# Four heads of num in the 64x64 quadrants of TensorE: a linear-attention and MLP kernel on one core

## The chip, the cores and the metric

The kernel runs on one core of a Trainium2 chip. The metric is the device time of a run in microseconds; lower is better. Times are medians over several runs, and a kernel is always timed in turns with the kernel before on the same chip.

Engine names in the profile: PE is TensorE (matmul), PEld its weight loads, DVE is VectorE, ACT is ScalarE, POOL is GpSimd, SP the engine that issues the output and spread DMAs. TensorE writes its results to `ps_all`, which the kernel divides into eight banks of 512 columns that are used in turn.

## The reference

In short form:

```python
batch, n_heads, seq, head_dim = 8, 8, 576, 64          # n_tokens 4608, d_model 512, d_ff 2048

def phi(x):
    return np.where(x > 0, x, np.exp(x) - 1.0) + 1.0
q_p, k_p = phi(q), phi(k)
kv  = einsum('bhsd,bhse->bhde', k_p, v)
z   = sum(k_p, axis=2)
num = einsum('bhsd,bhde->bhse', q_p, kv)
den = einsum('bhsd,bhd->bhs', q_p, z)[..., None] + 1e-06
x   = (num / den) -> [4608, 512]

h = x @ w_in
g = h - tanh(h)
out = g @ w_out                                        # float32, [4608, 512]
```

## The kernel before

The tokens are worked in nine chunks of 512. A chunk has a first dense layer (sixteen steps `s1` of four 128x128x512 matmuls) and a second (sixteen steps `s2` of four). The attention of a later batch is threaded between these steps. Batch 0 comes before chunk 0 in a prologue; batch 1 runs inside chunk 0, batch 2 inside chunk 1, and so on to batch 7 in chunk 6.

num of a pair of heads is one full 128x128 matmul: the two heads' kv stand as diagonal blocks of a 128x128 stationary operand, so half of the array multiplies zeros. Four matmuls of 512 columns and four of 64 (the last 64 of 576 tokens) make up a batch.

```python
    def load_wi(g):
        f0 = g * (DF // 4)
        nc.gpsimd.dma_start(out=w_in_sb[:, :, f0:f0 + DF // 4],
                            in_=moe_w_in[:, f0:f0 + DF // 4].rearrange("(ko ki) f -> ki ko f", ki=128))
    # ... (cut)
    def num_mm(b, p, banks):
        kz, qT = kz_t[b], qT_t[b]
        ps = banks().rearrange("p (j t) -> p j t", j=8)
        if p < NP:
            nc.tensor.matmul(ps, kz[:, p // 2, p % 2, 0:128], qT[:, p % 2, 0:8, p // 2, :], start=True, stop=True)
        else:
            for a in range(NP):
                nc.tensor.matmul(ps[:, a, :], kz[:, a // 2, a % 2, 0:128], qT[:, a % 2, 8, a // 2, :],
                                 start=True, stop=True)
        return ps
    # ... (cut: a_num multiplies a bank by the spread reciprocal rdb on VectorE; banks 6 and 7 in turn)
    def a_spread_pe(b, bank0, pairs):      # the spread of batches 0 and 1: selector times reciprocal, in fp32
        bp = ps_all[:, bank0:bank0 + 4, :]
        for n, p in enumerate(pairs):
            for t in range(4):
                r = slice(32 * t, 32 * t + 32)
                nc.tensor.matmul(bp[:, t, 144 * n:144 * n + 144], sel[r, p].rearrange("p h e -> p (h e)"),
                                 rden_t[b][r], start=True, stop=True)
        return bp
    # ... (cut)
    load_k(0); load_q(0); load_v(0)        # GpSimd's stream, in order
    make_identity(nc, ident)
    for g in range(4):
        load_wi(g)
    nc.gpsimd.memset(sel, 0.0)             # the selector of the spread
    for t in range(4):
        nc.gpsimd.affine_select(out=sel[32 * t:32 * t + 32], ...)
    load_k(1); load_wo(0); load_q(1); load_wo(1); load_v(1); load_wo(2); load_wo(3)
    # ... (cut: 36 matmuls of zeros, 0.43 us apart before the first clock record
    # at 6.09 us, 0.22 after it; phi of batch 0)
    a_qT_pe(0, 0, side)                    # transposes of q
    a_kv_half(0, 0, kvb)
    a_qT_pe(0, 1, side)
    a_kv_half(0, 1, kvb)
    a_den(0, Banks([0]))                   # ends in the reciprocal on VectorE
    ns0 = a_num_copy(0, Banks([1, 4, 5, 6, 7]))
    bp_a = a_spread_pe(0, 0, (0, 1))
    bp_b = a_spread_pe(0, 4, (2, 3))
    for p in range(NP):
        a_scale(0, p, ns0, (bp_a, bp_b)[p // 2], 144 * (p % 2))     # x = num * spread reciprocal
    # ... (cut) for batches 2 to 7, in the second layer of a chunk:
            for p in range(NP + 1):
                s2[9 + p].append(lambda p=p: a_num(n1, p))
```

kv runs in 64x128 tiles, den in 128x32 tiles and the spread in 32x128 tiles, so the array is already cut up there. The spread copies each token's reciprocal of den to the 64 rows of its head: for batches 0 and 1 by these matmuls, for later batches by DMA through DRAM.

Of the kernel before, what the change touches and what calls it, by code (L numbers as in the profile page):

```python
# [11 lines left out]
F32 = mybir.dt.float32  # L12
# [6 lines left out]
def kernel(  # L19
# [9 lines left out]
    nc = tc.nc  # L29
    B, H, S, D = q.shape  # L30
    N = B * S
    DM = H * D
    DF = moe_w_in.shape[1]
    NP = H // 2
    NF = DF // 128
    NC = N // 512
    J = S // 64
# [8 lines left out]
    rpool = ctx.enter_context(tc.tile_pool(name="rpool", bufs=2))  # L46
# [16 lines left out]
    attn = Banks([6, 7])  # L63
# [43 lines left out]

    def load_wi(g):
        f0 = g * (DF // 4)
        nc.gpsimd.dma_start(out=w_in_sb[:, :, f0:f0 + DF // 4],  # L110
                            in_=moe_w_in[:, f0:f0 + DF // 4].rearrange("(ko ki) f -> ki ko f", ki=128))

    def load_wo(g):
        nc.gpsimd.dma_start(out=w_out_sb[:, 4 * g:4 * g + 4, :],
# [28 lines left out]
            out=qT_t[b].rearrange("p i j g t -> p (i j) (g t)"),  # L143
            in_=qp_t[b].rearrange("p i j h d -> p (i j h d)"))

    def a_qT_pe(b, i, banks):
        if i == 0:
            new_qT(b)
        for n, (j0, j1) in enumerate(((0, 5), (5, 9))):
            ps = banks().bitcast(BF16).rearrange("p (j t) -> p j t", t=128)  # L150
            for j in range(j0, j1):
                nc.tensor.transpose(ps[:, j - j0, :], qp_t[b][:, i, j].rearrange("p h d -> p (h d)"), ident)  # L152
            src = ps[:, 0:j1 - j0, :]
            dst = qT_t[b][:, i, j0:j1].rearrange("p j g t -> p j (g t)")
            if n == 0:
                nc.scalar.copy(dst, src)
            else:
                nc.vector.tensor_copy(dst, src)
# [17 lines left out]
    def a_kv_half(b, i, banks):  # L176
        if i == 0:
            kz_t[b] = work.tile([128, 2, 2, 160], BF16, name="kz")
        ps = [banks()[:, 0:192] for hg in range(2)]
        kv_mm(b, i, ps)  # L180
        for hg in range(2):
            nc.vector.tensor_mul(kz_t[b][:, hg, i, :], ps[hg][:, 0:160], mask[:, hg, i, :])
# [30 lines left out]
                in_=ds[4 * hh:4 * hh + 4].rearrange("h t c -> (h t c)").partition_broadcast(64))  # L213
        rdb_t[b] = rdb

    def num_mm(b, p, banks):
        kz, qT = kz_t[b], qT_t[b]
        ps = banks().rearrange("p (j t) -> p j t", j=8)
        if p < NP:
            nc.tensor.matmul(ps, kz[:, p // 2, p % 2, 0:128], qT[:, p % 2, 0:8, p // 2, :], start=True, stop=True)  # L220
        else:
            for a in range(NP):
                nc.tensor.matmul(ps[:, a, :], kz[:, a // 2, a % 2, 0:128], qT[:, a % 2, 8, a // 2, :],
                                 start=True, stop=True)
        return ps

    def a_num(b, p):
        rdb = rdb_t[b]
        ps = num_mm(b, p, attn)
        if p < NP:  # L230
            nc.vector.tensor_mul(  # L231
                xT[:, p, S * b:S * b + 512].rearrange("p (j t c) -> p j t c", j=8, t=4),
                ps.rearrange("p j (t c) -> p j t c", t=4),
                rdb[:, p, :, 0:8, :].rearrange("p t j c -> p j t c"))
        else:
            nc.vector.tensor_mul(
                xT[:, :, S * b + 512:S * b + 576].rearrange("p a (t c) -> p a t c", t=4),
                ps[:, 0:NP, :].rearrange("p a (t c) -> p a t c", t=4), rdb[:, :, :, 8, :])

    def a_num_copy(b, banks):  # L240

        ns = rpool.tile([128, NP, J, 64], F32, name="ns", tag="rdb")
        ps = num_mm(b, NP, banks)
        nc.scalar.copy(ns[:, :, 8, :], ps[:, 0:NP, :])
        if b == 0:
            for p in range(NP):
                num_mm(b, p, banks)
            for p in (0, 2):
                nc.scalar.copy(ns[:, p:p + 2, 0:8, :].rearrange("p a j t -> p a (j t)"),
                               ps_all[:, 4 + p:6 + p, :])  # L250
        else:
            for p in range(NP):
                ps = num_mm(b, p, banks)
                nc.scalar.copy(ns[:, p, 0:8, :], ps)
        return ns

    def a_spread_pe(b, bank0, pairs):

# [7 lines that stand above are left out]
# [60 lines left out]
    for hh in range(2):  # L326
        nc.vector.memset(mask[64 * hh:64 * hh + 64, :, :, 64 * hh:64 * hh + 64], 1.0)
        for p in range(NP):
            m = 128 + 4 * hh + p
            nc.vector.memset(mask[64 * hh:64 * hh + 64, p // 2, p % 2, m:m + 1], 1.0)  # L330
    for i in range(2):
        nc.vector.memset(v_b[i][:, :, 2], 1.0)
# [16 lines left out]
    a_qT_pe(0, 0, side)  # L349
    a_kv_half(0, 0, kvb)  # L350
    a_qT_pe(0, 1, side)
    a_kv_half(0, 1, kvb)
    a_den(0, Banks([0]))
    ns0 = a_num_copy(0, Banks([1, 4, 5, 6, 7]))
    bp_a = a_spread_pe(0, 0, (0, 1))
    bp_b = a_spread_pe(0, 4, (2, 3))
    for p in range(NP):
        a_scale(0, p, ns0, (bp_a, bp_b)[p // 2], 144 * (p % 2))
    load_q(2)
    load_k(2)  # L360
    load_v(2)
# [1 line left out]
    for c in range(NC):  # L363
        gT = gpool.tile([128, NF, 512], BF16, name="gT")
        n1, n2 = c + 1, c + 2
        s1 = {i: [] for i in range(16)}
        s2 = {i: [] for i in range(16)}
        if c == 0:
            side = Banks([4, 5, 6, 7])
            sub = {}  # L370

            def spread1(h):
                sub["bp"] = a_spread_pe(1, 4, (2 * h, 2 * h + 1))
                for p in (2 * h, 2 * h + 1):
                    a_scale(1, p, sub["ns"], sub["bp"], 144 * (p % 2))

            s1[11].append(lambda: a_kphi(1, 0))
            s1[13].append(lambda: a_kphi(1, 1))
            s1[15].append(lambda: a_qphi(1, 0))
            s2[1].append(lambda: a_qphi(1, 1))  # L380
            s2[4].append(lambda: a_qT_pe(1, 0, side))
            s2[5].append(lambda: a_qT_pe(1, 1, side))
            s2[6].append(lambda: a_kv(1, side))
            s2[8].append(lambda: a_den(1, side))
            s2[9].append(lambda: (sub.update(ns=a_num_copy(1, side)), load_v(3)))
            s2[11].append(lambda: spread1(0))
            s2[13].append(lambda: spread1(1))
            s2[14].append(lambda: a_qphi(2, 0))
            s2[15].append(lambda: a_qphi(2, 1))
        elif n1 < B:  # L390
            s1[9 if c == 1 else 5].append(lambda: a_kv(n1, attn))
            s1[11 if c == 1 else 8].append(lambda: (a_den(n1, attn), a_spread(n1)))
            for p in range(NP + 1):
                s2[9 + p].append(lambda p=p: a_num(n1, p))
            if c + 3 < B:
                s1[10].append(lambda: load_v(c + 3))
        if c == 1:
            s1[1].append(lambda: a_kphi(2, 0))
            s1[3].append(lambda: (a_kphi(2, 1), load_k(3), load_q(3)))
            s1[5].append(lambda: a_qT_pe(2, 0, attn))  # L400
            s1[7].append(lambda: a_qT_pe(2, 1, attn))
        if c >= 1 and n2 < B:
            if c > 1:

                s1[0].append(lambda: (gate(gT, 0), load_k(n2), load_q(n2)))
            d = 4 if c == 1 else 2
            s2[d].append(lambda: a_kphi(n2, 0))
            s2[d + 2].append(lambda: a_kphi(n2, 1))
            s2[d + 4].append(lambda: a_qphi(n2, 0))
            s2[d + 6].append(lambda: (a_qphi(n2, 1), a_qT_dma(n2)))  # L410
        if c == 0:

            hs = [ps_all[:, fi, :] for fi in range(4)]
            first = Banks([4, 5, 6, 7, 0, 1, 2, 3])
            for p in range(NP):
                for fi in range(4):
                    l1mm(c, fi, hs[fi], p)
            for fi in range(4):
                l1act(fi, hs[fi], gT)
        for fi in range(4 if c == 0 else 0, NF):  # L420
            h = first() if c == 0 else dense()
            for p in range(NP):
                l1mm(c, fi, h, p)
            l1act(fi, h, gT)
            for f in s1[fi]:
                f()
        os_ = {}
        for s in range(16):

            (g, i) = divmod(s, 4) if c == 0 else (s % 4, s // 4)  # L430
            if g == 0:
                os_[i] = ps_all[:, i, :] if c == 0 else dense()
            l2mm(gT, os_[i], i, 4 * g, 4 * g + 4)
            if g == 3:
                evac(c, i, os_[i])
            for f in s2[s]:
                f()
# [30 lines left out]
```

## Time and profile before

| | |
|---|---|
| median time | 303.05 us (302.71 to 303.22, 3 runs) |
| span of the profiled run, granted clock | 301.5 us, 0.997 |
| TensorE busy | 292.2 us, 97% |
| first dense matmul | 20.06 us |
| num of one batch in the chain | 0.98 us |

The prediction shows the lines that carry the reading. One row of the page that it didn't show matters later: the granted clock in 40 equal slices, in tenths. The first is the row of the profiled kernel before. The second line below is from the view of busy time by stretch: the stretch in us, its length, then busy time and count of PE, PEld, DVE, ACT and POOL, the granted clock, the DMA share and GB/s.

```profile
PEclk9999999999999999999999999999999999999998
```

```profile
16.33:19.74 3.41, 2.93 (x40) 1.89 (x39) 2.21 (x3) 2.30 (x3) 3.33 (x6) 1.00 1.24 207
```

The reader should see that TensorE was busy for 2.93 of the 3.41 us ahead of the first dense matmul, and that the clock stayed full. The last digit of the row is 8 because the clock is recorded at half again from 299.64 us, after the last matmul; a run's mean clock of 0.997 therefore need not mean that any matmul ran slower.

### The profile page before, as it was taken

What the parts mean: (1) busy time and instruction counts of PE and PEld (TensorE: products, weight loads), DVE (VectorE), ACT (ScalarE), POOL (GpSimd) and SP (SyncE); (2) the same over time, 40 slices, a digit from 0 to 9 for tenths busy, and PEclk for the clock granted to TensorE, in tenths of its full rate; (3) what the DMA queues carried; (4) which work ended last, traced back from release to release, by engine and by line L of the source; (5) the groups of instructions that cost most, each with busy time, mean ns of one, the idle gap of its engine ahead of it and who ended that gap; (6) DMA issues with size and microseconds to landing.
All of it is one profiled execution on the core that took longest, in us unless ns stands there. A gap on an engine that the chain in (4) does not pass through costs nothing.

```text
span 301.5 us, 4703 instructions
## 1 busy us (share of the span) xinstructions
PE 292.2 (97%) x1790; PEld 138.7 (46%) x1790; DVE 180.0 (60%) x304; ACT 149.6 (50%) x228; POOL 51.7 (17%) x91
## 2 busy tenths in 40 slices
PE   8989999979999999999999999999999999999993
PEld 3544454444445444544454445444544444444441
DVE  7658944887557854785478556865681467008500
ACT  3637914954735653566256625662562166136420
POOL 8863253051006000600050003000000000000000
PEclk9999999999999999999999999999999999999998
DMA  6999999677879776967787777477108310130033
GB/s 95 193 206 206 205 207 206 171 113 139 214 101 188 147 170 139 152 109 200 142 145 128 192 149 125 85 177 148 38 2 193 71 35 0 37 86 18 2 70 70
DMA packets 36406, 38.23 MB, mean 127 GB/s; under 512 B 14432, under 2 KB 31008, under 8 KB 35616
## 3 DMA queue, kind: packets, MB, share of 16 engines
q0 software_dynamic: 17600, 18.35, 37.7%
q1 hardware_dynamic: 18784, 19.58, 28.9%
q8 instruction: 14, 0.23, 0.3%
q14 instruction: 8, 0.07, 0.1%
HBM read 43.78 MB, written 9.55 MB: 177 GB/s over the span
## 4 chain that ended last, share of the span: by engine, by line
PE 86%; DMA 4%; DVE 3%; ACT 2%; POOL 1%; issue 1%; SPq 0%; DVEq 0%; ACTq 0%; POOLq 0%
PE ps_all L275 39%; PE ps_all L290 38%; PE ps_all L165 4%; DMA out_dram<-osb 2%; PE ps_all L220 2%; DMA qraw<-in_q_dram 2%; ACT e L127 1%; DVE gT L281 1%; PE ps_all L190 1%; ACT osb L295 1%; PE ps_all L152 1%; POOL kraw L85 1%; PE ps_all L263 1%; DVE qp L129 1%; DVE kp L129 1%
## 5 line engine op out<-in xcount | busy, mean ns | idle before, releaser
L290 PE MATMUL ps_all<-w_out_sb,gT 128*128 128x512 bf16 x576 | 131.6, 379 | 0.0
L281 DVE TENSOR_TENSOR gT<-ps_all,th 128x512 bf16<-128x512 f32 x144 | 96.9, 687 | 53.6 <-ACT th L280 53.2
L275 PE MATMUL ps_all<-xT,w_in_sb 128*128 128x512 bf16 x576 | 128.2, 379 | 0.3 <-DVE xT L268 0.3
L280 ACT ACTIVATE th<-ps_all 128x512 f32<-128x512 f32 x144 | 85.2, 599 | 51.5 <-PE ps_all L275 46.8
L275 PEld LDWEIGHTS <-w_in_sb 128*128 128x128 bf16 x576 | 55.3, 98 | 66.6 <-issue 1.3
L290 PEld LDWEIGHTS <-gT 128*128 128x128 bf16 x576 | 55.6, 98 | 65.7 <-issue 0.3
L295 ACT COPY osb<-ps_all 128x512 f32<-128x512 f32 x36 | 21.1, 587 | 79.7 <-PE ps_all L290 59.6
L231 DVE TENSOR_TENSOR xT<-ps_all,rdb 128x512 bf16<-128x512 f32 x24 | 16.4, 689 | 11.8 <-PE ps_all L220 11.8
L104 POOL DMA_DIRECT2D v<-in_v_dram x32 | 19.2, 616 | 19.0 <-PE ps_all L165 6.0
L127 ACT ACTIVATE e<-kraw 128x1152 bf16<-128x1152 bf16 x16 | 18.5, 1165 | 5.3 <-DMA kraw<-in_k_dram 5.3
L129 DVE TENSOR_TENSOR kp<-e,r 128x1152 bf16<-128x1152 bf16 x16 | 12.2, 760 | 14.1 <-ACT e L127 13.0
L127 ACT ACTIVATE e<-qraw 128x1152 bf16<-128x1152 bf16 x16 | 18.4, 1166 | 0.6 <-DMA qraw<-in_q_dram 0.6
L129 DVE TENSOR_TENSOR qp<-e,r 128x1152 bf16<-128x1152 bf16 x16 | 12.1, 758 | 7.8 <-ACT e L127 7.0
L286 POOL COPY g<-gT 1x1 bf16<-1x1 bf16 x4 | 0.7, 176 | 92.9 <-DVE gT L281 92.9
L165 PE MATMUL ps_all<-v,kp 64*128 64x192 bf16 x288 | 13.7, 243 | 0.0
L165 PEld LDWEIGHTS <-kp 64*128 64x128 bf16 x288 | 11.5, 94 | 3.3 <-issue 2.5
L343 PE MATMUL ps_all<-zero 128*128 128x512 bf16 x36 | 10.3, 460 | 1.2 <-DVE zero L302 1.2
L220 PE MATMUL ps_all<-qT,kz 128*128 128x512 bf16 x32 | 11.2, 379 | 0.0
L89 POOL DMA_DIRECT2D kraw<-in_k_dram x14 | 8.7, 628 | 11.0 <-ACT th L280 9.6
L89 POOL DMA_DIRECT2D qraw<-in_q_dram x14 | 8.8, 642 | 6.1 <-DVE r L128 6.1
L268 DVE TENSOR_TENSOR xT<-ns,ps_all 128x576 bf16<-128x576 f32 x8 | 5.6, 749 | 5.2 <-PE ps_all L263 5.2
L174 DVE TENSOR_TENSOR kz<-ps_all,mask 128x320 bf16<-128x320 f32 x14 | 6.2, 486 | 3.7 <-PE ps_all L165 3.7
(46 smaller groups left out, 92.3 us busy)
## 6 DMA issues: line engine op xcount, KB each, us to landing
out_dram<-osb SPq DMA_DIRECT2D x72, 128.0 KB
rdb<-ds SPq DMA_DIRECT2D x12, 576.0 KB
v<-in_v_dram POOLq DMA_DIRECT2D x32, 144.0 KB, 6.4
kraw<-in_k_dram POOLq DMA_DIRECT2D x14, 288.0 KB, 5.1
qraw<-in_q_dram POOLq DMA_DIRECT2D x14, 288.0 KB, 7.0
w_in_sb<-in_moe_w_in_dram POOLq DMA_DIRECT2D x4, 512.0 KB, 10.1
w_out_sb<-in_moe_w_out_dram POOLq DMA_DIRECT2D x4, 512.0 KB, 13.2
kraw<-in_k_dram POOLq DMA_DIRECT2D x4, 144.0 KB, 3.7
```

What stands on the lines that cost most here:

```text
L89: nc.gpsimd.dma_start(out=t[64 * hg:64 * hg + 64].rearrange("p i h j d -> p (i h) (j d)"), in_=src[b, 4 * hg:4 * hg + 4].rearrange("h (p j ...
L104: nc.gpsimd.dma_start(out=v_b[b % 2][64 * hg:64 * hg + 64, i, 0:2].rearrange("p h j d -> p h (j d)"), in_=v[b, h0:h0 + 2].rearrange("h (p ...
L127: nc.scalar.activation(e, x, AF.Exp)
L129: nc.vector.tensor_tensor(store[b][:, i].rearrange("p j h d -> p h j d"), e, r, ALU.min)
L165: nc.tensor.matmul(ps[hg], kp[r, i, j].rearrange("p h d -> p (h d)"), vt[r, i, :, j, :], start=(j == 0), stop=(j == J - 1))
L220: nc.tensor.matmul(ps, kz[:, p // 2, p % 2, 0:128], qT[:, p % 2, 0:8, p // 2, :], start=True, stop=True)
L231: nc.vector.tensor_mul(xT[:, p, S * b:S * b + 512].rearrange("p (j t c) -> p j t c", j=8, t=4), ps.rearrange("p j (t c) -> p j t c", t=4), ...
L275: nc.tensor.matmul(h, w_in_sb[:, p, fi * 128:(fi + 1) * 128], xT[:, p, c * 512:(c + 1) * 512], start=(p == 0), stop=(p == NP - 1))
L280: nc.scalar.activation(th, h, AF.Tanh)
L281: nc.vector.tensor_sub(gT[:, fi, :], h, th)
L290: nc.tensor.matmul(o, gT[:, fi, i * 128:(i + 1) * 128], w_out_sb[:, fi, :], start=(fi == 0), stop=(fi == NF - 1))
L295: nc.scalar.copy(osb, o)
```

## The change

The intent is to use the whole array: kv's two 64x64 blocks of a pair go one above the other in one column half of the array, and those of another pair in the other half, so that four heads run side by side in one pass and num takes two passes of 512 columns where it took four. The outputs then come in another order of heads, so the rows of w_in are regrouped to match, which cuts each of its four loads in two. In the prologue the first half of num goes ahead of the second half of kv. The transposes of batch 2's q in chunk 1 are spread over four steps instead of two. The core of the diff (the mask's index, the splitting of the transposes' helper, `a_num_copy` and the lines that the new ones replace in num are cut):

```diff
     def load_wi(g):
         f0 = g * (DF // 4)
-        nc.gpsimd.dma_start(out=w_in_sb[:, :, f0:f0 + DF // 4],
-                            in_=moe_w_in[:, f0:f0 + DF // 4].rearrange("(ko ki) f -> ki ko f", ki=128))
+        for hg in range(2):
+            nc.gpsimd.dma_start(
+                out=w_in_sb[64 * hg:64 * hg + 64, :, f0:f0 + DF // 4],
+                in_=moe_w_in[256 * hg:256 * hg + 256, f0:f0 + DF // 4].rearrange("(c e) f -> e c f", e=64))
 ...
+    def num_mm(b, i, ps):
+        kz, qT = kz_t[b], qT_t[b]
+        for ii, j0, j1, o in ((i, 0, 8, 0),) if i < 2 else ((0, 8, 9, 0), (1, 8, 9, 64)):
+            for hg in range(2):
+                for hh in range(2):
+                    r, c = slice(64 * hh, 64 * hh + 64), slice(64 * hg, 64 * hg + 64)
+                    nc.tensor.matmul(ps[hh][c, o:o + 64 * (j1 - j0)], kz[r, hg, ii, r],
+                                     qT[r, ii, j0:j1, hg, :], start=True, stop=True)
+    def a_num(b, i):
+        rdb = rdb_t[b]
+        ps = [attn(), attn()]            # both banks 6 and 7
+        num_mm(b, i, ps)
+        # ... one multiplication on VectorE for each bank
 ...
     a_qT_pe(0, 1, side)
+    ns0 = new_ns(0)
+    a_num_copy(0, ns0, 0, side)
     a_kv_half(0, 1, kvb)
     a_den(0, Banks([0]))
-    ns0 = a_num_copy(0, Banks([1, 4, 5, 6, 7]))
-    bp_a = a_spread_pe(0, 0, (0, 1))
-    bp_b = a_spread_pe(0, 4, (2, 3))
+    a_num_copy(0, ns0, 2, Banks([1, 2]))
+    a_num_copy(0, ns0, 1, side)
+    bp_a = a_spread_pe(0, 0, (0,))
+    bp_b = a_spread_pe(0, 4, (1, 2, 3))
 ...
+            def num1():                  # batch 1, in chunk 0
+                sub["ns"] = new_ns(1)
+                for i in (2, 0, 1):
+                    a_num_copy(1, sub["ns"], i, side)
+                load_v(3)
 ...
-            for p in range(NP + 1):
-                s2[9 + p].append(lambda p=p: a_num(n1, p))
+            for i in range(3):
+                s2[9 + 2 * i].append(lambda i=i: a_num(n1, i))
 ...
-            s1[5].append(lambda: a_qT_pe(2, 0, attn))
-            s1[7].append(lambda: a_qT_pe(2, 1, attn))
+            for n in range(4):
+                s1[4 + n].append(lambda n=n: a_qT_pe(2, n // 2, attn, (n % 2,)))
```

## The prediction

> **What bounds the kernel now.** I read the page first (engine shares, chain), then the chain in order of time, then the timelines of TensorE, VectorE and GpSimd over the first 50 us, and last the waits. The page and the waits:

> ```profile
> PE 292.2 (97%) x1790; PEld 138.7 (46%) x1790; DVE 180.0 (60%) x304; ACT 149.6 (50%) x228; POOL 51.7 (17%) x91
> ...
> L220 PE MATMUL ps_all<-qT,kz 128*128 128x512 bf16 x32 | 11.2, 379 | 0.0
> ...
> PE ps_all L152 <- DVE qT L158: 1.1, 1, 1.1
> ```

> TensorE is busy 97% of a 301.5 us span at a granted clock of 0.997, and num (line 220) never waits. The reader should see that VectorE and ScalarE have slack on average, so a microsecond of TensorE time is a microsecond of the kernel, unless it lies where TensorE waits anyway. The chain in order of time says where that is:

> ```profile
> 17.54 0.95 PE ps_all L263 x14
> ...
> 18.59 1.43 DVE xT L268 x2
> ...
> 20.06 13.97 PE ps_all L275 x64
> ...
> 81.35 0.21 PE ps_all L220
> 81.56 0.86 PE ps_all L290 x4
> 82.42 0.22 PE ps_all L220
> ...
> 84.58 0.22 PE ps_all L220
> 84.80 0.86 PE ps_all L290 x4
> 85.66 0.12 PE ps_all L223 x4
> ```

> From 20.06 us to the last dense matmul the chain is TensorE nearly without a break (the exception is around 53 to 63 us in chunk 1, where the page's waits show TensorE waiting for the transposed q of batch 2). A dense 128x512 matmul costs 13.97/64 = 0.218 us of the chain (0.86/4 = 0.215 later). num of one batch costs four times 0.215 plus 0.12 for the four 64-column matmuls: 0.98 us. For the six batches 2 to 7 that is 5.9 us, for batch 1 another 0.98, and batch 0 lies in the prologue. That is everything that the quadrants can halve: about 3.5 us, or 1.1%.

> What the quadrants cost is in the timeline, at the places where the kernel already leaves the full array:

> ```profile
> 42.65 1.90 PE L290 MATMUL ps_all<-w_out_sb,gT 128*128 128x512 bf16 x8
> ...
> 44.48 0.43 PE L190 MATMUL ps_all<-qT,kz 128*32 128x144 bf16 x16
> ...
> 44.85 1.04 PE L290 MATMUL ps_all<-w_out_sb,gT 128*128 128x512 bf16 x4
> ```

> Eight dense matmuls from 42.65 at 0.216 would end their issue at 44.38; the 128x32 matmuls start at 44.48, so 0.09 us goes on entering. Sixteen matmuls of 144 columns in four column tiles are four rounds; at the 2.37 columns a nanosecond of a dense matmul (512 in 0.216 us) a round is 0.061 us, together 0.24. They hold TensorE 44.48 to 44.85 = 0.37. So leaving costs 0.12 to 0.13, and a visit to another tiling about 0.21 us besides its rounds. kv (64x128) gives the same: 1.59 us in the chain for 18 rounds of 0.081 = 1.46 leaves 0.13, with another 0.09 on entry. The four tiles of a round are truly concurrent, with four different moving operands, so I expect the four quadrants to be as well.

> [...]

> **The change part by part.**

> Steady batches 2 to 7. Two full matmuls (0.43 us) become one visit of four concurrent 64x64 matmuls: 0.22 for the round, 0.21 for entering and leaving, minus nothing: 0.42 to 0.43. This is no gain, twice per batch, because the visits stand alone between groups of four dense matmuls. The tail columns now need a third visit: two rounds of 64 columns, 0.03 plus about 0.05[...], plus 0.21: 0.29 us where four full matmuls took 0.12. Per batch 0.43 + 0.43 + 0.29 = 1.15 against 0.98: +0.15 to +0.17; six batches about +0.9 us.

> Chunk 1 (num of batch 2). Each visit now fills both banks 6 and 7 and needs both evicted (2 x 0.67 us on VectorE) before the next, two steps later (8 x 0.216 + 0.43 = 2.16 us). Before, VectorE took its first num of batch 2 at 82.01, 0.8 us after TensorE had begun it, and between the second and third it did 1.2 us of q's phi. With pairs, visit 2's evictions fall at about 84.5 to 85.9 and visit 3 wants bank 7 at 85.6: a stall of about +0.3 us. In chunks 2 to 5 the phi work is two steps earlier and the same reckoning leaves about 0.2 us to spare: 0. The later chunk has no phi: 0.

> Batch 1 (chunk 0). The three parts share one visit: 0.21 + 0.08 + 2 x 0.22 = 0.73 against 0.98, a gain of 0.25. But they go through a ring of four banks, two at a time, in the order 2, 0, 1: part 1 takes the banks of part 2 and must wait for ScalarE's two small copies. These start some 0.24 us after the matmul (now 45.81 to 46.04) and take about 0.2 us each, so part 1 can go some 0.45 us later than it could. Net +0.2 us.

> Prologue. num of batch 0's first half goes in front of kv's second half: its eviction (two copies of 0.6 us) leaves the critical stretch, but kv, den and the reciprocal come some 0.37 us later (one round of 0.22, one more switch). The spread is now split so that only its first quarter stands before the first scale, and the first dense matmul needs banks 0 to 3 free of one scale (0.75 us) instead of two (1.43 us). By TensorE, VectorE and ScalarE alone I get the first dense matmul at about 19.5 instead of 20.06: -0.55 us.

> But w_in's four DMAs become eight of 64 partitions, in GpSimd's stream ahead of the selector of the spread:

> ```profile
> 9.99 3.00 POOL L110 DMA_DIRECT2D w_in_sb<-in_moe_w_in_dram  x4
> ...
> 12.97 0.56 POOL L311 MEMSET sel<- 128x512 f32 x1
> ...
> 13.61 2.84 POOL L314 TENSOR_SCALAR_AFFINE_SELECT sel<-sel 32x512 f32<-32x512 f32 x4
> ...
> 17.51 0.95 PEld L263 LDWEIGHTS ps_all<-rden,sel 32*128 32x128 f32 x20 [0.63 <-issue]
> ```

> A DMA of this shape costs about 0.62 us (1.27 for two at 16.40), so eight take 5 us instead of 3; the last four also reuse the semaphores of v's loads, the last of which lands at 14.4. GpSimd is then free at about 15.2 instead of 12.97, and the selector, 3.47 us of work, is ready at about 18.7 instead of 16.45. The reciprocal is ready at 17.4 + 0.37 = 17.8, so the spread waits 0.9 us for the last 32 rows of the selector. First quarter of the spread done 19.35, scale until 20.2, first dense matmul at 20.25: +0.2 us instead of -0.55. The bytes of w_in and the DMA engines' rate do not change, and its first quarter lands at 17.3, so its data are not late.

> Splitting batch 2's transposes over four steps in chunk 1: TensorE waits there for copies that stand in VectorE's queue behind two gT subtractions; the last copy keeps its place in that queue, so the end of the stretch stays: 0.

> Sum: +0.9 + 0.3 + 0.2 + 0.2 = +1.6 us on 303.05, that is 304.65. I take 304.5, since the selector's delay is the least certain part and its absence would give back 0.75.

> **The rivals.** (a) The full halving: the quadrants cost no switch[...]. For it: num would be 7 x 0.5 = 3.5 us shorter, and with the prologue's 0.55 the time would be 299. Against it: every change of tiling in the trace, at kv, den and the spread alike, shows the gap. (b) The quadrants run only two at a time[...]: each of 14 rounds costs another 0.22: +3 us, some 307.5. Against it: den's four column tiles and kv's two row tiles both run together at full rate; no run shows both at once. (c) The selector is not late, because GpSimd issues the half-sized DMAs in about 0.4 us each: 303.9. For it: v's smaller DMAs pitch 0.58, so hardly. (d) The stalls on paired banks are larger than reckoned, in every chunk: 0.3 us x 6 instead of x 1, 306.

> **Range and chances.** The four terms have perhaps 0.3 to 0.4 us of doubt each, the state of the run 0.25. Range 302.6 to 305.9. Two per cent would be 6 us: more than all of num can give, and more than (b). Faster 0.01, within 2% 0.97, slower 0.02.

> **What would show it.** In the changed profile: num's matmuls 64*64 with 16 of 512 columns' worth of rounds in the chain, each lone visit about 0.42 us and the tail visit about 0.29; the next dense matmul 0.3 us after the last quadrant's start; a wait of a quadrant on VectorE's num in chunk 1 and on ScalarE's copy of ns in chunk 0; a wait of the spread's weights on POOL line 314 near 18 us; the first dense matmul near 20.2. The prediction is wrong if visits take 0.25 us (rival a), if four quadrants take 0.65 (rival b), or if the first dense matmul starts before 19.7.

0.9 + 0.3 + 0.2 + 0.2 came to +1.6 us. One term, the "about 0.05" us of the tail's second round, was the author's estimate without a trace behind it, some 0.3 us of the sum in six batches; in the changed kernel the second round of the tail visit near 118.7 us starts 0.053 us after the first.

## The result and the profile after

The changed kernel is slower: 306.51 us median (305.37 to 307.06, 4 runs) against 302.92 (302.71 to 303.22, 4 runs), a ratio of 1.0113 with a 95% interval of 1.0083 to 1.0143. Ratios here are the mean time of one kernel's runs over the mean of the other's runs in the same rounds, so they are not quite the ratio of the medians quoted. The sign of the prediction was right, the size was not: +1.45 us predicted (with +1.6 as its sum), +3.6 measured, outside its range.

The page of the changed kernel, its clock row and num's group (line 226 is now num, 276 and 291 the dense layers, 264 the spread, 315 the selector):

```profile
PE 295.3 (97%) x1854; PEld 136.7 (45%) x1854; DVE 179.3 (59%) x310; ACT 149.6 (49%) x232; POOL 53.7 (18%) x95
...
PEclk9989999999999999999999999999999999999999
...
L226 PE MATMUL ps_all<-qT,kz 64*64 64x512 bf16 (+1 forms) x128 | 8.6, 300 | 0.1
```

One digit of the clock row differs: the third slice, 15.2 to 22.9 us, reads 8 instead of 9. The chain of the changed kernel, in order of time:

```profile
18.71 0.52 PE ps_all L264 x5
...
20.14 15.66 PE ps_all L276 x64
...
47.84 0.26 ACT ns L256
...
83.31 0.34 PE ps_all L226 x4
83.64 1.83 PE ps_all L291 x8
...
114.44 0.34 PE ps_all L226 x4
114.78 1.83 PE ps_all L291 x8
...
118.78 0.19 PE ps_all L226 x8
118.97 1.83 PE ps_all L291 x8
```

The first 64 dense matmuls take 15.66 us where they took 13.97. Eight dense matmuls after a visit of num take 1.83, where eight at 0.216 would take 1.73. So a lone visit costs 0.34 + 0.10 = 0.44 us in place of two full matmuls at 0.43, and the tail visit 0.19 + 0.10 = 0.29 in place of 0.12.

The timeline around the first dense matmul (start, length, what; in brackets the idle time before it and what ended it):

```profile
15.21 0.54 POOL L312 MEMSET sel<- 128x512 f32 x1
...
15.82 2.84 POOL L315 TENSOR_SCALAR_AFFINE_SELECT sel<-sel 32x512 f32<-32x512 f32 x4
...
17.79 0.55 PEld L264 LDWEIGHTS ps_all<-rden,sel 32*128 32x128 f32 x6 [1.12 <-POOL sel L315]
...
20.84 0.15 PEld L276 LDWEIGHTS <-w_in_sb 128*128 128x128 bf16 x1 [0.27 <-issue]
21.27 0.15 PEld L276 LDWEIGHTS <-w_in_sb 128*128 128x128 bf16 x1 [0.28 <-issue]
21.69 0.15 PEld L276 LDWEIGHTS <-w_in_sb 128*128 128x128 bf16 x1 [0.28 <-issue]
```

The selector is ready only at 18.7 us and the spread waits for it, as predicted. Then the weights of successive dense matmuls are loaded 0.43 us apart, twice the usual 0.216: TensorE runs at half clock. The view of busy time by stretch names the window:

```profile
16.86:20.28 3.42, 2.23 (x37) 1.77 (x34) 1.76 (x3) 1.35 (x4) 3.29 (x6) 1.00 1.20 196
```

```profile
20.10:23.70 3.60, 3.56 (x9) 1.31 (x9) 2.04 (x3) 0.00 (x0) 1.72 (x3) 0.53 1.24 203
```

Reading the same places of both chains gives the whole difference:

| place in the chain | before, us | after, us | later by |
|---|---|---|---|
| first dense matmul | 20.06 | 20.14 | 0.08 |
| second layer of chunk 0 | 34.03 | 35.80 | 1.77 |
| first spread of batch 1, after its num | 48.59 | 50.56 | 1.97 |
| kv of batch 2, in chunk 1 | 65.36 | 67.32 | 1.96 |
| chunk 2, after num of batch 2 | 87.51 | 89.82 | 2.31 |
| chunk 3, after num of batch 3 | 118.28 | 120.80 | 2.52 |
| chunk 7, after num of batch 7 | 241.38 | 244.71 | 3.33 |
| last sixteen matmuls before the final copies | 282.82 | 286.15 | 3.33 |

So: 0.08 for the later start, 1.69 for the half clock, 0.20 for batch 1, 0.35 for batch 2 and about 0.20 for each of five later batches. Without the half clock that is 1.64 us.

### The profile page after: what moved, and what is told of

Same layout as the page of the kernel before. It is cut to its first block, busy times and chain, and to the rows that moved or that the text cites. A ratio compares the mean times of both kernels' runs of the same rounds, so it can differ in the third digit from the quotient of the medians.

```text
span 304.8 us, 4853 instructions
## 1 busy us (share of the span) xinstructions
PE 295.3 (97%) x1854; PEld 136.7 (45%) x1854; DVE 179.3 (59%) x310; ACT 149.6 (49%) x232; POOL 53.7 (18%) x95
## 4 chain that ended last, share of the span: by engine, by line
PE 85%; DMA 6%; DVE 2%; ACT 2%; POOL 1%; issue 1%; SPq 0%; DVEq 0%; POOLq 0%
PE ps_all L276 40%; PE ps_all L291 38%; PE ps_all L168 4%; DMA out_dram<-osb 2%; DMA w_in_sb<-in_moe_w_in_dram 2%; PE ps_all L226 2%; DMA kraw<-in_k_dram 2%; DVE gT L282 1%; ACT osb L296 1%; PE ps_all L193 1%; ACT e L129 1%; POOL sel L315 1%; PE ps_all L264 1%; POOL kraw L85 1%; DVE kp L131 0%
## 5 line engine op out<-in xcount | busy, mean ns | idle before, releaser
L276 PE MATMUL ps_all<-xT,w_in_sb 128*128 128x512 bf16 x576 | 130.2, 383 | 0.2 <-DVE xT L269 0.2
L291 PE MATMUL ps_all<-w_out_sb,gT 128*128 128x512 bf16 x576 | 130.1, 379 | 0.0
L291 PEld LDWEIGHTS <-gT 128*128 128x128 bf16 x576 | 54.4, 98 | 65.8 <-issue 3.1
L236 DVE TENSOR_TENSOR xT<-ps_all,rdb 128x512 bf16<-128x512 f32 x24 | 15.4, 683 | 11.0 <-PE ps_all L226 11.0
L226 PE MATMUL ps_all<-qT,kz 64*64 64x512 bf16 (+1 forms) x128 | 8.6, 300 | 0.1
```

The costliest lines, as they stand in the source:

```text
L226: nc.tensor.matmul(ps[hh][c, o:o + 64 * (j1 - j0)], kz[r, hg, ii, r], qT[r, ii, j0:j1, hg, :], start=True, stop=True)
L236: nc.vector.tensor_mul(xT[:, 2 * i + hh, S * b:S * b + 512].rearrange("p (j t c) -> p j t c", j=8, t=4), ps[hh].rearrange("p (j t c) -> p ...
L276: nc.tensor.matmul(h, w_in_sb[:, p, fi * 128:(fi + 1) * 128], xT[:, p, c * 512:(c + 1) * 512], start=(p == 0), stop=(p == NP - 1))
L291: nc.tensor.matmul(o, gT[:, fi, i * 128:(i + 1) * 128], w_out_sb[:, fi, :], start=(fi == 0), stop=(fi == NF - 1))
```

## The experiments

The theory after the result: (1) splitting w_in's loads keeps GpSimd busy longer, the selector comes late, TensorE idles ahead of the spread, and the clock falls for one window; (2) each lone visit of the quadrants pays a pair of tiling switches. The rivals: the half clock comes from the quadrants or the shorter num themselves; or the quadrants are slow for another reason than the switch.

The first four kernels ran together on one chip, with the kernel before at 303.20 us (302.43 to 304.06, 11 runs).

### The kernel before with split loads

```diff
# on the kernel before
-        nc.gpsimd.dma_start(out=w_in_sb[:, :, f0:f0 + DF // 4], in_=...)
+        for hf in range(2):
+            nc.gpsimd.dma_start(out=w_in_sb[64 * hf:64 * hf + 64, :, f0:f0 + DF // 4],
+                                in_=...[64 * hf:64 * hf + 64])        # same rows as before
```

> The kernel before, with only the loads of w_in cut into eight DMAs of 64 partitions (old row order, old num). Theory 1 (GpSimd's longer issue makes the selector late, TensorE then idles before the spread, and the clock falls to half for one window of 3.4 us after it): first dense matmul 0.3 to 0.6 us later than 20.06, the first 8 or 9 dense matmuls at 427 ns apart, time 304.8 to 305.3 (+1.9 to +2.4 us). Theory 2 (the half clock comes from the quadrants or from the shorter num of batch 0, not from the selector): no half-rate dense matmuls, time 303.2 to 303.5.

The line numbers of the profile differ a little from kernel to kernel. Measured: 305.22 us median (303.62 to 305.97, 6 runs), ratio 1.0059 (1.0034 to 1.0084). Timelines of this kernel, GpSimd and TensorE, then the stretch ahead of its dense layer:

```profile
10.09 5.28 POOL L111 DMA_DIRECT2D w_in_sb<-in_moe_w_in_dram  x8
...
15.97 2.85 POOL L316 TENSOR_SCALAR_AFFINE_SELECT sel<-sel 32x512 f32<-32x512 f32 x4
```

```profile
18.87 1.24 PE L265 MATMUL ps_all<-rden,sel 32*128 32x144 f32 x26 [0.22 <-POOL sel L316]
```

```profile
17.35:20.76 3.41, 2.37 (x33) 1.84 (x33) 1.16 (x3) 1.64 (x2) 3.28 (x7) 1.00 1.24 205
```

With the old num and no quadrant at all, the loads take 5.28 us of GpSimd instead of 3.00, the spread waits for the selector, and the clock is recorded at half from 20.76 to 24.18 us, where dense matmuls start 427 ns apart. Of the six runs four have a mean clock of 0.994 (304.84 to 305.97 us) and two of 1.000 (304.58 and 303.62). So the split loads alone bring the half clock, in four runs of six; the quadrants are not needed for it. The rest is the later start: the first recorded dense matmul is at 21.20 us instead of 20.06, later than the 0.3 to 0.6 expected, since here it waits for two scales.

### The selector between the loads

```diff
-    for g in range(4):
+    for g in range(2):
         load_wi(g)
     nc.gpsimd.memset(sel, 0.0)
     ... affine_select of sel ...
+    for g in range(2, 4):
+        load_wi(g)
```

> The changed kernel, with the selector built between the second and third quarter of w_in, so that it is ready before the reciprocal. Theory 1: no wait of the spread on GpSimd, first dense matmul at about 19.5, all dense matmuls at 216 ns from the start, time 304.2 (-2.3 us against the changed kernel: 1.7 of the clock, 0.6 of the earlier start). Theory 2: first dense matmul at 19.5 but still 8 or 9 of them at 427 ns, time 305.9.

Measured: 305.79 us median (305.18 to 307.46, 6 runs), ratio 1.0099 (1.0074 to 1.0123). The time was missed, the mechanism was not. The spread no longer waits for GpSimd, the first recorded dense matmul is at 19.25 us, and all six clocks are 0.997 to 0.999. The gain is lost again 18 us later:

```profile
37.76 1.02 PE L291 MATMUL ps_all<-w_out_sb,gT 128*128 128x512 bf16 x4 [1.08 <-DMA w_out_sb<-in_moe_w_out_dram]
```

The second quarter of w_out lands at 37.72 us; in the kernel before it landed at 37.33 and TensorE reached it at about 37.5. The loads keep the DMA engines at some 205 GB/s from 15 to 53 us (the page's row of the kernel before), so an earlier start of the dense layer only reaches this landing earlier. How much is lost here differs from run to run: in the ten other profiles the same quarter landed between 35.7 and 37.5 us, and only this one shows the wait. Another 0.5 us goes in chunk 1, where the spread reciprocal of batch 2 lands at 83.0 us, after the first visit, and the second and third visit wait for their paired banks. My estimate of some 0.6 us for the earlier start was therefore not to be had in this run, and the median of six shows no sign of it either.

### Matmuls of zeros in the wait

```diff
     a_num_copy(0, ns0, 1, side)
+    for n in range(8):
+        nc.tensor.matmul(ps_all[:, 3, :], zero[:, 0:128], zero, start=True, stop=True)
     bp_a = a_spread_pe(0, 0, (0,))
```

> The changed kernel, with eight matmuls of zeros (1.7 us) put in TensorE's stream where it waits for the spread; the selector stays late, so the start stays where it is. Theory 1: first dense matmul at 20.1 to 20.4 but at full clock, time 304.8 to 305.1 (-1.4 to -1.7 us). Theory 2 (the quadrants as such[...]): half clock as before, 306.5 to 306.8.

Measured: 305.24 us median (304.82 to 305.91, 6 runs), ratio 1.0072 (1.0054 to 1.0089). TensorE's timeline of this kernel:

```profile
16.93 1.67 PE L360 MATMUL ps_all<-zero 128*128 128x512 bf16 x7 [0.16 <-issue]
18.53 1.29 PE L264 MATMUL ps_all<-rden,sel 32*128 32x144 f32 x32
20.08 5.12 PE L276 MATMUL ps_all<-xT,w_in_sb 128*128 128x512 bf16 x22 [0.26 <-DVE xT L269]
```

The dense layer starts at the same time as in the changed kernel, but at full clock; the last matmul issues at 297.85 us where it did at 299.58. All six of its clocks are 0.996 to 0.998. So neither the late start nor the quadrants alone halve the clock: here it turned on what TensorE did in the wait. Whether idle time as such is what counts, this run cannot tell (see what stays open, below). This is the changed kernel without its half clock, and it is 0.72% slower than the kernel before: the part that the prediction had priced.

With four matmuls instead of eight:

```diff
-    for n in range(8):
+    for n in range(4):
```

> The changed kernel with four instead of eight matmuls of zeros in the wait (0.9 us). If the clock falls when TensorE's busy time in one 3.4 us window is too low (2.2 us in the changed kernel, 2.9 in the kernel before, which kept its clock), 2.2 + 0.9 = 3.1 us keeps the clock: 304.8 to 305.3, as with eight. If all of the wait must be filled: half clock in part of the runs, 305.8 or more in the median, with a wider spread.

Measured (with the kernel before at 303.18 us, 302.57 to 303.85, 11 runs): 305.19 us median (304.89 to 306.84, 6 runs), ratio 1.0075 (1.0054 to 1.0096), clocks 0.996 to 1.000. Half the filling keeps the clock as well. The slowest of its runs, at clock 1.000, is the profiled one, and it shows what else spreads the times of the quadrants. TensorE, then VectorE, in chunk 1:

```profile
82.00 0.41 PE L226 MATMUL ps_all<-qT,kz 64*64 64x512 bf16 x4
...
84.92 0.37 PE L226 MATMUL ps_all<-qT,kz 64*64 64x512 bf16 x1 [0.68 <-DVE xT L236]
85.52 0.41 PE L226 MATMUL ps_all<-qT,kz 64*64 64x512 bf16 x3 [0.23 <-DVE xT L236]
```

```profile
84.18 1.29 DVE L236 TENSOR_TENSOR xT<-ps_all,rdb 128x512 bf16<-128x512 f32 x2 [1.35 <-DMA rdb<-ds]
```

The spread reciprocal lands 2 us after the first visit has filled banks 6 and 7, so the second visit waits for each bank in turn: its first matmul starts 0.75 us late and the other three another 0.60 later. In the changed kernel's own profile the same DMA landed 0.6 us after the first visit and the third visit lost 0.15.

### One visit per batch

```diff
-            for i in range(3):
-                s2[9 + 2 * i].append(lambda i=i: a_num(n1, i))
+            s2[9].append(lambda: a_num_all(n1))
+    def a_num_all(b):
+        pp = {}
+        for i, banks in ((2, dense), (0, attn), (1, dense)):   # two more pairs from the dense banks
+            pp[i] = [banks(), banks()]
+            num_mm(b, i, pp[i])
+        for i in range(3):
+            a_num(b, i, pp[i])                                 # a_num without its own matmuls
```

> The changed kernel, with the three parts of num of batches 2 to 7 in one visit (tail and second part in two pairs of the dense banks), so 6 switches of tiling instead of 18 there. If a switch pair costs 0.21 us whatever it encloses: each batch 0.72 instead of 1.16 us (chunk 1 1.31), time -2.6 to -2.8 us against the changed kernel, 303.8, with the half-clock stretch still there. Rival (the quadrants' cost is not the switch but slow or serial matmuls): -0.5 us or less.

Measured: 303.27 us median (302.18 to 305.74, 6 runs), ratio 1.0010 (0.9978 to 1.0041), 0.8 to 1.0% below the changed kernel's (1.0113 above, 1.0091 later). TensorE's timeline in chunk 1:

```profile
80.84 1.89 PE L297 MATMUL ps_all<-w_out_sb,gT 128*128 128x512 bf16 x8
82.66 0.69 PE L226 MATMUL ps_all<-qT,kz 64*64 64x64 bf16 x16
83.28 5.35 PE L297 MATMUL ps_all<-w_out_sb,gT 128*128 128x512 bf16 x23
```

All sixteen quadrant matmuls of a batch hold TensorE from 82.66 to 83.28, and with entry and exit about 0.72 us, less than the 0.98 of the full array. The quadrants do run four at a time at full rate; what they cost in the changed kernel was being visited three times. The edit also gives two of the three parts other banks, but in the changed kernel's chunks 2 to 6 no visit waited for a bank (0.34 and 0.19 us each in the chain), so that is not where the gain comes from. The ratio to the changed kernel is taken across jobs, not in turns. The half clock is still there in the profiled run (18.51 to 21.92 us, clock 0.994). The slowest run, 305.74 us, has a mean clock of 0.986, low enough for two such windows; it has no trace.

### Both cures together

```diff
+ the eight matmuls of zeros
+ a_num_all in one visit
```

> The changed kernel with both cures: eight matmuls of zeros in TensorE's wait for the spread, and num of batches 2 to 7 in one visit per batch. If the two causes (half clock 1.7 us, 12 switch pairs at 0.21 us) are separate, they add: first dense matmul about 20.1 at full clock, last matmul about 294.8, time 301.5 to 302.0, faster than the kernel before by 0.4 to 0.6%. Rival (the one-visit kernel was fast only because its half-clock window fell early): no gain over it, 303.

Measured: 302.22 us median (301.59 to 302.63, 6 runs), ratio 0.9967 (0.9951 to 0.9982), last matmul at 295.46 us in a profile whose dense layer began at 20.59. The two causes add up: every one of the six clocks is 0.996 to 0.998, and the version is faster than the kernel before by 0.33%, a little less than expected (301.5 to 302.0).

### The transposes in two steps again

```diff
-            for n in range(4):
-                s1[4 + n].append(lambda n=n: a_qT_pe(2, n // 2, attn, (n % 2,)))
+            s1[5].append(lambda: a_qT_pe(2, 0, attn))
+            s1[7].append(lambda: a_qT_pe(2, 1, attn))
```

> The changed kernel with the transposes of batch 2's q again in two steps of chunk 1 instead of four. My prediction's view (the last copy keeps its place behind gT in VectorE's queue, so the stretch ends at the same time): same as the changed kernel within 0.2 us, TensorE's two waits there again sum to about 2.1 us. Rival (the split hides part of the wait): 0.5 us or more slower than the changed kernel.

Measured: 306.60 us median (304.35 to 307.38, 6 runs), ratio 1.0094 (1.0064 to 1.0125). The ratio of the changed kernel, 1.0113 and 1.0091, is on both sides of it, but the intervals, some 0.3% either way, could not show the rival's 0.5 us; the traces have to decide. In its trace TensorE's two waits for the transposes are 0.78 and 1.29 us, in the changed kernel's 1.15 and 0.92: 2.07 us both. From the start of chunk 1's first layer to kv it is 11.80 us in both. The split moves the wait and does not shorten it.

### The changed kernel once more, and a later place for the transposes

Run together, with the kernel before at 303.05 us (302.83 to 303.92, 11 runs). The first is the changed kernel unaltered:

> The changed kernel once more, unaltered, with more rounds than the first result had. [...]some of six runs keep the clock (mean granted clock 0.997 or more, about 305.2 us) and most lose it (0.991 to 0.995, 306.4 to 307.1); if it always falls in full, all six lie at 306.4 to 307.1.

The two outcomes weighed were a clock that some of the runs keep and one that every run loses.

Measured: 306.19 us median (304.78 to 307.45, 6 runs), ratio 1.0091 (1.0063 to 1.0118). Run by run, time and mean clock go together: 306.53, 305.86, 307.45 and 306.71 us at 0.991 to 0.993, 305.07 at 0.995, 304.78 at 1.000. A window of 3.41 us at half clock takes 1.71 us from a span of some 303, so a run that has one cannot show more than 0.9944: the run at 0.995 kept its clock as well (the half clock after the last matmul is enough for that), and the line at 0.997 in the expectation was drawn too high. Two runs of six kept the clock. The four that lost it average 306.64, 1.7 us over the two that kept it, which is the cost that the chain shows. By the same rule one of the four runs of the first result, 305.37 us at 0.995, had kept it. So the changed kernel pays for the half clock in some runs only: four of six here, three of four in the first result. That the place of the window makes the difference is an estimate, from the first change at 4.65 to 7.11 us in the profiles; it was not shown, as no run of the changed kernel that kept its clock has a trace.

The second goes on from both cures:

```diff
# in chunk 1 only
-                s1[4 + n].append(lambda n=n: a_qT_pe(2, n // 2, attn, (n % 2,)))
+                s1[10 + n].append(lambda n=n: a_qT_pe(2, n // 2, attn, (n % 2,)))
# kv from s1[9] to s1[14], den from s1[11] to s1[15], load_v from s1[10] to s1[15], num from s2[9] to s2[11]
```

> The eight matmuls of zeros and the one-visit num, and in chunk 1 the transposes of batch 2's q moved from steps 4 to 7 to steps 10 to 13 (kv to 14, den to 15, num to step 11 of the second layer), where VectorE's backlog should be gone. If TensorE's 2.1 us of waits there come from that backlog alone: 1.5 to 2 us less than with both cures, 300.3 to 300.8. Rival (the spread of the reciprocals through DRAM, 12 us from den to landing, is then too late, or the waits only move): 302 or more.

Measured: 302.15 us median (301.28 to 302.64, 6 runs), ratio 0.9962 (0.9947 to 0.9977). The waits at the transposes fall from 2.07 to 0.4 us (kv then waits another 0.4 for the last copy), and in the profiled run, also the fastest, the last matmul is at 294.25 us; but the reciprocal then lands at 84.6 us, VectorE's multiplications come late, and the dense layer of chunk 2 waits 0.65 us at 86.2. The ratio differs from that of both cures (0.9967) by much less than either interval, so no further gain is shown. The rival was right.

## Why the prediction was wrong, point by point

- **The bound.** Right. TensorE sets the end: every delay in the table is still there at the last matmul, and even chunk 1's waits absorbed none of it (+1.97 before them, +1.96 after).
- **The switch of tiling: 0.21 us per visit, 0.43 per lone visit, 0.29 for the tail.** Right: 0.44 and 0.29. The gap in the traces is 0.09 us on the way in and 0.09 to 0.12 on the way out, counted from the last start of a round, for 64x64, 64x128 and 128x32 tiles alike. (Its 0.24 us for sixteen 144-column matmuls was reckoned, not read: the sixteen starts span 0.21 us, with those of one round 3 to 4 ns apart. The reading stands.) The steady batches were +0.15 to +0.17 by the prediction and +0.20 by the chain; six batches, +0.9 predicted, +1.2 measured without the stall. The kernel with one visit shows that the number of visits is the cause: 0.72 us a batch where three visits took 0.44 + 0.44 + 0.29.
- **Chunk 1's stall, +0.3.** Right in kind, uncertain in size. It is 0.15 us in the changed kernel's profile and 1.35 in one of four matmuls of zeros. It depends on when the spread reciprocal lands, which the prediction left out; it named VectorE's phi work alone.
- **Batch 1, +0.2.** Right: +0.20, with the predicted wait for ScalarE's small copies in the chain (0.26).
- **The prologue, +0.2.** The start is right: predicted 20.25, measured 20.14, with the predicted wait for the selector. This is the step that failed, though: the term was priced as a delay of TensorE alone, at an unchanged clock. With the wait that it named the clock also fell for 3.41 us, which cost 1.69 us in the profiled run. Splitting w_in's loads in the kernel before brings it without the quadrants (clock 0.994 in four of six runs); filling the wait takes it away without moving the start (0.996 to 0.998 in six, the dense layer at 20.08 us).
- **The transposes' split, 0.** Right: 2.07 us of waits either way.
- **The rivals.** None came true. A lone visit takes 0.44 us, so the switch is not free (a), and four quadrants in one round take 0.34, not the 0.65 of quadrants two at a time (b). The eight DMAs held GpSimd from 9.81 to 15.21 us, so the selector was late (c). Stalls on paired banks came in chunk 1 alone, so (d), whose 306 lies nearest the measured time, is near by luck. The prediction also said that without the selector's delay 0.75 us would come back. In the kernel that tried it nothing came back: in its profile the second quarter of w_out landed too late for an earlier start to count.
- **Sum.** Predicted +1.6; by the chain all terms but the half clock add up to +1.64, partly by luck, as the switches cost 0.3 more and the start and the stall together 0.3 less. The changed kernel without its half clock (matmuls of zeros in the wait) is at +2.2 by its ratio, 305.24 us and inside the range; the half clock takes the changed kernel's median out of it.

What stays open: what makes the recorded clock fall. In five profiles the window that lost the clock had 2.23 to 2.39 us of 3.41 busy, by the profile's busy time. But the kernel with the selector between the loads kept it at 2.38, and the kernel before kept it in chunk 1, in its window from 60.71 to 64.12 us, with only 1.66 us busy and a wait of 1.1 us (longest gap between matmul starts 1.35 us, against 1.23, from 16.59 to 17.82 us, before the fall in the changed kernel). So neither busy time nor the length of a gap decides alone. The windows differ in what TensorE was busy with: in the changed kernel, in the window before the fall, 32 of the 33 recorded matmul starts are the spread's, in 32x128 tiles; in chunk 1 all are dense matmuls and transposes in 128x128 tiles. Whether that matters was not shown; no run tested it.

Why the reciprocal of batch 2 lands at different times in different runs is open as well. A regrouped quarter of w_in in one DMA, which would have spared GpSimd the longer issue, is in no run, so that direct test is missing.

## What to carry to other kernels

Count the visits to a tiling, not only the matmuls in it: here a visit that replaces two full matmuls breaks even (0.44 us for 0.43), and one that replaces eight wins (0.72 for 0.98). When a change adds idle time to TensorE just ahead of a dense stretch, add a possible half-clock window to its price (1.7 us here), and look at the granted clock run by run; matmuls of zeros in the wait were a cheap test here, and a cure (four or eight of them: 0.996 to 1.000 in twelve runs). A saving at the start can be lost at the next landing, as here: the dense layer began 0.9 us earlier (19.25 us for 20.14), then waited 1.08 us for w_out's second quarter, with the loads at some 205 GB/s.
